# Stages 1 and 3 of a DFT in blocks of three instead of two, in a kernel of spectral mixing and hash-routed experts

## The chip, the cores and the metric

One NeuronCore of a Trainium2 chip runs the whole program. The metric is device time in microseconds for one execution. TensorE (PE in the profile) multiplies matrices: the stationary operand is loaded by a weight load (PEld), the moving operand streams through in columns, and the result lands in PSUM. VectorE (DVE), ScalarE (ACT) and GpSimd (POOL) do the other arithmetic. SyncE (SP), ACT and POOL issue DMAs; all DMAs run on the core's 16 DMA engines.

## The reference

```python
def _attn_ref(x, filt_r, filt_i):              # x: (8, 2496, 256) float32
    X = np.fft.rfft(x, axis=1)
    F = (filt_r + 1j * filt_i)[None, :, :]     # (1249, 256)
    return np.fft.irfft(X * F, n=x.shape[1], axis=1).astype(np.float32)

def _moe_ref(x, token_ids, w1, w2):            # x: (19968, 256), 8 experts, F = 1024
    expert_idx = token_ids * np.int64(2654435761) % np.int64(8)
    for e in range(8):
        mask = expert_idx == e
        out[mask] = np.maximum(x[mask] @ w1[e], 0.0) @ w2[e]
    return out
```

The first function's output, reshaped to 19968 tokens, is the second function's x. Everything is float32.

## The kernel before, in words

**The transform.** The length 2496 is split as 39 x 64 (N1 = 39, N2 = 64). The position in the sequence is s = 64 n1 + n2, and each batch goes through three stages (class `Batch`, lines 160 to 254).

- Stage 1 (lines 177 to 188) is a DFT of 39 points over n1, for each n2. Its input is real, so 20 frequencies with a real and an imaginary part (40 rows) come out. A matrix of 39 x 40 is small for an array of 128 x 128, so two blocks of n2 (n2 below 32 and from 32 on) are put on the diagonal of one stationary matrix `wf_t` of 78 x 80. A piece `u` (eight of them per batch) loads `x` for four values of n2 in each block (line 175, one DMA, 78 rows of 4 KB), does two products of 512 columns (line 185, two n2 times 256 channels each), copies them out of PSUM on ACT (line 187) and stores them to a DRAM buffer `d1` laid out as 40 x 64 x 256 (line 188).
- Stage 2 (lines 190 to 235) loads `d1` back with n2 on the rows (line 194), two DMAs per group of four frequencies, multiplies by a matrix that holds twiddles and the 64-point DFT (`pb`, line 202), by the filter (line 207, DVE), by the inverse matrix (`pc`, line 221), copies on ACT and stores to a second DRAM buffer `d2` of the same layout (line 228). There are 10 steps of forward and 10 of inverse work per batch.
- Stage 3 (lines 237 to 254) loads `d2` (line 239), does the inverse 39-point DFT with the 80 x 78 matrix `wi_t` (line 249), copies on DVE into a tile `o` (line 251) whose last 16 columns hold the token's number (an iota on POOL, line 245), and scatters one n2 at a time: 78 token rows per indirect DMA (line 257), four per piece and 32 per batch, to their places in the expert-sorted buffer `xs`. The index of each row stands in `sidx`.

A float32 product is two matmul instructions in the profile, each with its own weight load.

**Routing.** Early on, DVE and small matmuls count the tokens per expert, give each token a slot and write the slots to DRAM (line 403), from where they come back as `sidx` (line 404).

**Experts.** 163 tiles of 128 token rows follow. For tile i the kernel issues the load of tile i + 4's rows (line 519, SP), does the first layer (`up`, line 538), then conditional loads of the next weights (lines 283 and 285, SP), the transposes of tile i + 1 (line 527), then pieces of the transform that are due, then the second layer (`down`, line 550) and the scatter of the results (line 554, POOL).

**The order.** It is written by hand. Lists of (due time, piece) are sorted: `pre` (lines 491 to 496) runs before the first expert tile, and `main` (lines 498 to 504) is consumed tile by tile (lines 572 and 573), with due times in tiles. `part1` and `part3` (lines 462 and 479) spread the NU pieces of a stage evenly over a stretch of due times and issue each piece's load 1.9 steps ahead. Before the first expert tile run stage 1 of batches 0 to 2, stage 2 of batches 0 to 2 and stage 3 of batches 0 and 1; stage 1 of batch 3 and stage 3 of batch 2 come in the first six tiles, and the rest follows until tile 101. The expert tiles come in four groups that need the tokens of 2, 4, 6 and 8 batches. Buffers: three for `x`, two for `t1`, four for `t2`, three for `t4`, two for `o`, four PSUM tiles for all transform products. Each engine's and each queue's instructions run in the order in which they are written.

Of the kernel before, what the change touches and what calls it, by code (L numbers as in the profile page):

```python
# [19 lines left out]
P = 128  # L20
# [5 lines left out]

N1, N2 = 39, 64
NS, NQ = N1 // 2 + 1, 64
NR = 2 * N1
NK = 4 * NS  # L30
SG = 4
XG = 4
NU = N2 // 2 // XG
# [27 lines left out]
def dft_tables():  # L61
# [4 lines left out]
    wf = np.zeros((N1, 2, 2, NS, 2))  # L66
    wi = np.zeros((2, NS, 2, N1, 2))
# [27 lines left out]
def route_table():  # L95


    t = np.zeros((P, G + 2 + NQP), np.float32)
    p = np.arange(P)
    for g, b in enumerate(STAGES):  # L100
# [3 lines left out]
    t[:, G + 2:] = p[:, None] * NQP + np.arange(NQP)  # L104
    return t
# [3 lines left out]
def kernel(  # L109
# [42 lines left out]
    sidx = keep.tile([NR, B, N2 // 2], I32)  # L152
# [7 lines left out]
    class Batch:  # L160
# [8 lines left out]
        def rows(self, base, u):  # L169
            return bass.AP(tensor=base.tensor, offset=base.offset + (self.b * S + XG * u) * C,  # L170
                           ap=[[32 * C, NR], [C, XG], [1, C]])

        def load1(self, u):
            self.x[u] = xpool.tile([NR, XG, C], F32, name=f"x_{self.b}_{u}", tag="x")
            nc.sync.dma_start(out=self.x[u][:], in_=self.rows(x, u))

        def stage1(self, u):
            if self.d1 is None:
                self.d1 = dpool.tile([2 * NS, N2, C], F32, name=f"d1_{self.b}", tag="d1")
                self.d1_rows = self.d1.rearrange("a (h n) c -> (a h) n c", h=2)  # L180
            xt = self.x.pop(u)
            t1 = t1pool.tile([NK, XG, C], F32, name=f"t1_{self.b}_{u}", tag="t1")
            for i in range(XG // 2):
                ps = fps.tile([P, 2, C], F32, name=f"pa_{self.b}_{u}_{i}", tag="f")
                nc.tensor.matmul(out=ps[0:NK], lhsT=wf_t[:], rhs=xt[:, 2 * i:2 * i + 2, :],  # L185
                                 start=True, stop=True)
                nc.scalar.copy(out=t1[:, 2 * i:2 * i + 2, :], in_=ps[0:NK])  # L187
# [22 lines left out]
        def back(self, u):  # L210
            if self.d2 is None:
                self.d2 = dpool.tile([2 * NS, N2, C], F32, name=f"d2_{self.b}", tag="d2")
                self.d2_rows = self.d2.rearrange("a (h n) c -> (a h) n c", h=2)
# [23 lines left out]
        def load4(self, u):  # L237
            self.t4[u] = t4pool.tile([NK, XG, C], F32, name=f"t4_{self.b}_{u}", tag="t4")
            nc.sync.dma_start(out=self.t4[u][:], in_=self.d2_rows[:, XG * u:XG * u + XG, :])

        def stage3(self, u):

            t4 = self.t4.pop(u)
# [3 lines left out]
            for i in range(XG // 2):  # L247
                ps = fps.tile([P, 2, C], F32, name=f"pd_{self.b}_{u}_{i}", tag="f")
                nc.tensor.matmul(out=ps[0:NR], lhsT=wi_t[:], rhs=t4[:, 2 * i:2 * i + 2, :],  # L249
                                 start=True, stop=True)  # L250
                nc.vector.tensor_copy(out=o[:, 2 * i:2 * i + 2, 0:C], in_=ps[0:NR])  # L251
# [44 lines left out]
    rt = rpool.tile([P, G + 2 + NQP], F32)  # L296
    nc.scalar.dma_start(out=rt[:], in_=r_dram.ap())
    nc.scalar.dma_start(out=d_t[:], in_=d_dram.ap())
# [29 lines left out]
    def count():  # L328
# [26 lines left out]
        rv.update(mask=mask, run=run, ends=ends, ps=ps)  # L355

    def route():
# [36 lines left out]
        for g in range(1, G):  # L394
# [4 lines left out]
        slot = rpool.tile([P, NJ], F32)  # L399
        nc.vector.tensor_reduce(slot[:], acc[:].rearrange("p e j -> p j e"), axis=AX.X, op=OP.add)  # L400
        slot_i = rpool.tile([P, NJ], I32)
        nc.vector.tensor_copy(slot_i[:], slot[:])
        nc.gpsimd.dma_start(out=slot_dram[:].rearrange("(p j) -> p j", p=P), in_=slot_i[:])
        nc.gpsimd.dma_start(out=sidx[:], in_=slot_dram[:].rearrange("(b p n) -> p b n", b=B, p=NR))
# [13 lines left out]
                                       rt[:, G + 2:], op0=OP.mult, op1=OP.add)  # L418
        some = rpool.tile([P, NQP], F32)
        for e in range(E):  # L420
            nc.vector.tensor_scalar(some[:], rt[:, G + 2:], prior[:, e:e + 1], held[:, e:e + 1],
# [183 lines left out]
```

## Time and profile before

| what | value |
|---|---|
| median of 3 runs | 1742.96 us (1742.59 to 1743.45) |
| profiled execution | 1736.04 us |
| its span, first to last instruction | 1734.3 us |
| mean granted TensorE clock | 0.981 |
| DMA traffic | 260.72 MB, mean 150 GB/s |

The profile is one execution. Busy time is the union of an engine's instructions; a matmul's end is modelled, so its separate duration overlaps its neighbour's, and the distance between starts or the chain of waits is the better measure of what one costs. The chain is followed back from the last instruction, at each step to what released it. Stretches are counted from the first instruction.

### The profile page before, as it was taken

The numbers are of one execution on the slowest core, as the hardware profiler recorded it, in microseconds if no ns is written. First come the engines' busy times: TensorE is split into PE (matmuls) and PEld (weight loads), VectorE is DVE, ScalarE is ACT, GpSimd is POOL, SyncE is SP. The second block draws the span as 40 slices with busy tenths as digits, with TensorE's granted clock in tenths as the row PEclk, the third lists the DMA queues.
The fourth block names the chain that finished last, engine by engine and source line by source line (L and its number), as shares of the span: only waits on it lengthen the run. The fifth ranks groups of instructions, "written<-read, shape, count | busy, mean of one in ns | idle before, by whom it ended". The sixth has DMA issues, their size and how long they took to land.

```text
span 1734.3 us, 27336 instructions
## 1 busy us (share of the span) xinstructions
PE 1658.3 (96%) x9630; PEld 1390.2 (80%) x9630; DVE 462.6 (27%) x848; ACT 223.0 (13%) x373; POOL 428.3 (25%) x509
## 2 busy tenths in 40 slices
PE   5889869899999999999999999999999999999998
PEld 1455537588778888888888988888899999999997
DVE  8133412222332222222232232222222222222221
ACT  1322011121111111111110100000000000000000
POOL 1116434200233023321232222333321111111111
PEclk9999969899999999999999999999999999999999
DMA  9889755655766585375463554443516222222220
GB/s 249 230 204 318 202 145 170 168 158 157 218 199 174 160 239 183 93 210 131 118 189 103 176 179 131 130 129 119 163 43 232 87 87 86 86 84 85 84 82 11
DMA packets 158098, 260.72 MB, mean 150 GB/s; under 512 B 18271, under 2 KB 120192, under 8 KB 157643
## 3 DMA queue, kind: packets, MB, share of 16 engines
q1 hardware_dynamic: 108459, 166.93, 33.8%
q0 software_dynamic: 21168, 48.63, 8.7%
q10 hardware_dynamic: 28336, 43.43, 8.7%
q8 instruction: 77, 1.26, 0.3%
q14 instruction: 58, 0.48, 0.1%
HBM read 433.78 MB, written 86.09 MB: 300 GB/s over the span
## 4 chain that ended last, share of the span: by engine, by line
PE 64%; issue 24%; DMA 7%; POOL 4%; DVE 0%; POOLq 0%; SPq 0%; ACT 0%; ACTq 0%; DVEq 0%
PE ups L538 20%; PE dps L550 20%; PE pc L221 7%; PE pa L185 6%; PE pd L249 6%; PE pb L202 4%; POOL out_dram L554 4%; DMA x<-in_x_dram 2%; PE xps L527 1%; DMA w<-in_moe_w_dram 1%; DMA xs<-o,sidx 1%; DMA t<-d 1%; POOL xs L257 1%; DMA d<-g 1%; DVE o L251 0%
## 5 line engine op out<-in xcount | busy, mean ns | idle before, releaser
L538 PEld LDWEIGHTS ups<-xt,w 128*128 128x128 f32 x5216 | 610.5, 193 | 9.3 <-DVE xt L529 0.9
L538 PE MATMUL ups<-xt,w 128*128 128x128 f32 x5216 | 611.2, 276 | 0.5 <-DVE xt L529 0.5
L550 PE MATMUL dps<-w,ht 128*128 128x256 f32 x2608 | 591.8, 380 | 0.0
L550 PEld LDWEIGHTS dps<-w,ht 128*128 128x128 f32 x2608 | 490.5, 191 | 86.0 <-issue 24.5
L554 POOL DMA_INDIRECT out_dram<-osb,xg x163 | 159.9, 981 | 856.9 <-DVE osb L553 836.7
L257 POOL DMA_INDIRECT xs<-o,sidx x256 | 241.0, 942 | 399.9 <-issue 260.7
L544 DVE TENSOR_SCALAR ht<-ups 128x512 f32<-128x512 f32 x163 | 112.7, 691 | 525.7 <-PE ups L538 525.7
L542 ACT ACTIVATE ht<-ups 128x512 f32<-128x512 f32 x163 | 97.3, 597 | 1031.0 <-PE ups L538 1001.3
L553 DVE COPY osb<-dps 128x256 f32<-128x256 f32 x163 | 69.2, 424 | 507.7 <-PE dps L550 503.2
L185 PE MATMUL pa<-x,wf_t 78*80 78x512 f32 x256 | 144.8, 697 | 26.1 <-DMA x<-in_x_dram 26.0
L221 PE MATMUL pc<-p,e_t 128*128 128x256 f32 x640 | 154.6, 385 | 0.8 <-DVE p L207 0.8
L221 PEld LDWEIGHTS pc<-p,e_t 128*128 128x128 f32 x640 | 123.9, 194 | 21.7 <-DVE p L207 2.2
L207 DVE TENSOR_TENSOR p<-pb,filt 128x512 f32<-128x512 f32 x160 | 102.9, 685 | 113.5 <-PE pb L202 113.3
L249 PE MATMUL pd<-t,wi_t 80*78 80x512 f32 x256 | 125.8, 614 | 7.4 <-DMA t<-d 5.2
L185 PEld LDWEIGHTS pa<-x,wf_t 78*80 78x80 f32 x256 | 41.9, 171 | 91.9 <-issue 75.3
L251 DVE COPY o<-pd 78x512 f32<-78x512 f32 x128 | 87.2, 686 | 96.5 <-issue 41.4
L202 PE MATMUL pb<-t,d_t 128*128 128x256 f32 x320 | 89.0, 404 | 21.0 <-DMA t<-d 19.8
L202 PEld LDWEIGHTS pb<-t,d_t 128*128 128x128 f32 x320 | 61.8, 202 | 54.6 <-issue 39.3
L187 ACT COPY t<-pa 80x512 f32<-80x512 f32 x128 | 73.1, 581 | 183.7 <-PE pa L185 157.2
L249 PEld LDWEIGHTS pd<-t,wi_t 80*78 80x78 f32 x256 | 37.6, 153 | 57.7 <-issue 49.5
L224 ACT COPY g<-pc 128x512 f32<-128x512 f32 x80 | 46.8, 585 | 280.8 <-PE pc L221 255.3
L527 PE MATMUL xps<-ident,xg 128*128 128x128 f32 x326 | 62.5, 274 | 9.7 <-DMA xg<-xs 9.7
(80 smaller groups left out, 183.5 us busy)
## 6 DMA issues: line engine op xcount, KB each, us to landing
w<-in_moe_w_dram SPq DMA_DIRECT2D x326, 1024.0 KB
xg<-xs SPq DMA_DIRECT2D x163, 136.0 KB
d<-t ACTq DMA_DIRECT2D x64, 320.0 KB
t<-d SPq DMA_DIRECT2D x80, 256.0 KB
d<-g ACTq DMA_DIRECT2D x80, 256.0 KB
t<-d SPq DMA_DIRECT2D x64, 320.0 KB
x<-in_x_dram SPq DMA_DIRECT2D x64, 312.0 KB
xs<-o,sidx POOLq DMA_INDIRECT x256, 3.0
```

The lines of the kernel that those rows point to most:

```text
L185: nc.tensor.matmul(out=ps[0:NK], lhsT=wf_t[:], rhs=xt[:, 2 * i:2 * i + 2, :], start=True, stop=True)
L202: nc.tensor.matmul(out=ps[:, i, :], lhsT=d_t[:, s, :], rhs=self.t2[s // SG][:, s % SG, :], start=True, stop=True)
L207: nc.vector.tensor_tensor(out=pt[:], in0=ps[:], in1=f_t[k][:, 2 * u:2 * u + 2, :], op=OP.mult)
L221: nc.tensor.matmul(out=ps[:, i, :], lhsT=e_t[:, k, 2 * u + i, :], rhs=pr[k][:, i, :], start=(k == 0), stop=(k == 1))
L249: nc.tensor.matmul(out=ps[0:NR], lhsT=wi_t[:], rhs=t4[:, 2 * i:2 * i + 2, :], start=True, stop=True)
L251: nc.vector.tensor_copy(out=o[:, 2 * i:2 * i + 2, 0:C], in_=ps[0:NR])
L257: st = nc.gpsimd.indirect_dma_start(out=xs[:], out_offset=bass.IndirectOffsetOnAxis(ap=index, axis=0), in_=rows, in_offset=None, bounds_ch ...
L538: nc.tensor.matmul(out=ps[:, k, :], lhsT=w1[:, dp, fp * P:(fp + 1) * P], rhs=xt[i][:, dp, :], start=(dp == 0), stop=(dp == DP - 1))
L542: nc.scalar.activation(out=dst, in_=ps[:], func=AF.Relu)
L544: nc.vector.tensor_scalar_max(dst, ps[:], 0.0)
L550: nc.tensor.matmul(out=ps[:], lhsT=ht[:, fp, :], rhs=w2[:, fp, :], start=(fp == 0), stop=(fp == FP - 1))
L554: st = nc.gpsimd.indirect_dma_start(out=out[:], out_offset=bass.IndirectOffsetOnAxis(ap=xg[i][:, C:C + 1].bitcast(I32), axis=0), in_=o[:], ...
```

## The change

Stages 1 and 3 work on three values of n2 at once instead of two: the diagonal has three blocks and the matrices are 117 x 120 and 120 x 117. The blocks are now neighbouring values, n2 = 3 j + h with h = 0, 1, 2 and j = 0 to 20; n2 = 63 is left over and is done alone, with the first block of the same matrix (39 x 40). A piece takes four values of j, so there are six pieces per batch: five of four j, and one of one j and the single n2, which does two products of 256 columns. `x` is loaded by one DMA per block (three per piece, 39 rows each), and by a fourth in the last piece. The DRAM buffers `d1` and `d2` have n2 first (64 x 40 x 256). So stage 2 loads and stores 64 rows of 4 KB, and stages 1 and 3 store and load 120 rows of up to four runs of 1 KB. Token numbers come from a table (`tokno`) by a tensor_scalar on POOL in place of the iota. `sidx` is twice as wide and is filled by three DMAs. Each scatter holds 117 rows (21 per batch) or 39 (one per batch). Stage 2's arithmetic, the due times of the lists and the expert part stay.

```diff
-NR = 2 * N1
-NK = 4 * NS
+H, HN = 3, 21
+NR = H * N1
+NK = 2 * H * NS
 SG = 4
 XG = 4
-NU = N2 // 2 // XG
+NU = (HN + XG) // XG
...
-    for h in range(2):
-        wf[:, h, :, :, h] = w
-        wi[:, :, h, :, h] = v.transpose(0, 2, 1) / S
+    for h in range(H):
+        wf[h, :, h] = w
+        wi[h, :, :, h] = v.transpose(0, 2, 1) / S
...
-    sidx = keep.tile([NR, B, N2 // 2], I32)
+    sidx = keep.tile([NR, B, N2], I32)
+    tokno = keep.tile([NR, HN + 1], F32)
...
         def load1(self, u):
-            self.x[u] = xpool.tile([NR, XG, C], F32, name=f"x_{self.b}_{u}", tag="x")
-            nc.sync.dma_start(out=self.x[u][:], in_=self.rows(x, u))
+            xt = self.x[u] = xpool.tile([NR, XG, C], F32, name=f"x_{self.b}_{u}", tag="x")
+            off, n = x.offset + self.b * S * C, min(XG, HN - XG * u)
+            for h in range(H):
+                nc.sync.dma_start(out=xt[N1 * h:N1 * h + N1, 0:n, :],
+                                  in_=bass.AP(tensor=x.tensor, offset=off + (H * XG * u + h) * C,
+                                              ap=[[N2 * C, N1], [H * C, n], [1, C]]))
+            if n < XG:
+                nc.sync.dma_start(out=xt[0:N1, n, :],
+                                  in_=bass.AP(tensor=x.tensor, offset=off + (N2 - 1) * C, ap=[[N2 * C, N1], [1, C]]))
+
+        def products(self, w, rows, cols, src, dst, copy, u, name):
+            last = XG * u + XG > HN
+            for i in range(1 if last else XG // 2):
+                ps = fps.tile([P, 2, C], F32, name=f"{name}_{self.b}_{u}_{i}", tag="f")
+                if last:
+                    for k, f in enumerate((H, 1)):
+                        nc.tensor.matmul(out=ps[0:cols * f, k, :], lhsT=w[0:rows * f, 0:cols * f],
+                                         rhs=src[0:rows * f, k, :], start=True, stop=True)
+                        copy(out=dst[0:cols * f, k, 0:C], in_=ps[0:cols * f, k, :])
+                else:
+                    nc.tensor.matmul(out=ps[0:cols * H], lhsT=w[:], rhs=src[:, 2 * i:2 * i + 2, :],
+                                     start=True, stop=True)
+                    copy(out=dst[:, 2 * i:2 * i + 2, 0:C], in_=ps[0:cols * H])
+
+        def pieces(self, d, t, u):
+            n = min(XG, HN - XG * u)
+            main = d[0:H * HN].rearrange("(j h) a c -> (h a) j c", h=H)
+            parts = [(main[:, XG * u:XG * u + n, :], t[:, 0:n, :])]
+            if n < XG:
+                parts.append((d[N2 - 1], t[0:2 * NS, n, :]))
+            return parts
...
         def stage1(self, u):
-                self.d1 = dpool.tile([2 * NS, N2, C], F32, name=f"d1_{self.b}", tag="d1")
+                self.d1 = dpool.tile([N2, 2 * NS, C], F32, name=f"d1_{self.b}", tag="d1")
...
-            nc.scalar.dma_start(out=self.d1_rows[:, XG * u:XG * u + XG, :], in_=t1[:])
+            self.products(wf_t, N1, 2 * NS, self.x.pop(u), t1, nc.scalar.copy, u, "pa")
+            for dram, chip in self.pieces(self.d1, t1, u):
+                nc.scalar.dma_start(out=dram, in_=chip)
...
                 nc.sync.dma_start(out=t2[64 * p:64 * p + 64, :, :],
-                                  in_=self.d1[a0:a0 + SG, :, :].rearrange("s n c -> n s c"))
+                                  in_=self.d1[:, a0:a0 + SG, :])
...
-                    nc.scalar.dma_start(out=self.d2[a0:a0 + SG, :, :].rearrange("s n c -> n s c"),
+                    nc.scalar.dma_start(out=self.d2[:, a0:a0 + SG, :],
                                         in_=self.g[64 * p:64 * p + 64, :, :])
...
         def load4(self, u):
-            nc.sync.dma_start(out=self.t4[u][:], in_=self.d2_rows[:, XG * u:XG * u + XG, :])
+            for dram, chip in self.pieces(self.d2, self.t4[u], u):
+                nc.sync.dma_start(out=chip, in_=dram)
 
         def stage3(self, u):
-            nc.gpsimd.iota(o[:, :, C:].bitcast(I32), pattern=[[1, XG], [0, W - C]],
-                           base=self.b * S + XG * u, channel_multiplier=N2 // 2)
...
-            for i in range(XG):
+            nc.gpsimd.tensor_scalar(o[:, 0:n, C:].bitcast(I32),
+                                    tokno[:, XG * u:XG * u + n].unsqueeze(2).to_broadcast([NR, n, W - C]),
+                                    float(self.b * S), None, op0=OP.add)
+            self.products(wi_t, 2 * NS, N1, self.t4.pop(u), o, nc.vector.tensor_copy, u, "pd")
+            for i in range(n):
                 j = XG * u + i
-                scatter(o[:, i, :], sidx[:, self.b, j:j + 1], f"xs_{self.b}")
+                r, k = (NR, H * j) if j < HN else (N1, N2 - 1)
+                scatter(o[0:r, i, :], sidx[0:r, self.b, k:k + 1], f"xs_{self.b}")
...
-        nc.gpsimd.dma_start(out=sidx[:], in_=slot_dram[:].rearrange("(b p n) -> p b n", b=B, p=NR))
+        for h in range(H):
+            n = N2 if h == 0 else H * (HN - 1) + 1
+            slots = slot_dram[:]
+            nc.gpsimd.dma_start(out=sidx[N1 * h:N1 * h + N1, :, 0:n],
+                                in_=bass.AP(tensor=slots.tensor, offset=slots.offset + h,
+                                            ap=[[N2, N1], [S, B], [1, n]]))
```

## Rows read from the trace of the kernel before

**Rows 1.** The page, part 1: busy time, share of the span, instructions.
```profile
PE 1658.3 (96%) x9630; PEld 1390.2 (80%) x9630; DVE 462.6 (27%) x848; ACT 223.0 (13%) x373; POOL 428.3 (25%) x509
```

**Rows 2.** Busy time by stretch: us, engines (instructions), TensorE clock, DMA share, GB/s.
```profile
0.00:55.00 55.00, 33.59 (x40) 8.98 (x40) 35.98 (x66) 13.03 (x18) 13.95 (x27) 1.00 0.91 250
55.00:105.00 50.00, 45.18 (x151) 29.96 (x152) 13.92 (x25) 15.98 (x26) 0.00 (x0) 1.00 0.79 203
105.00:184.00 79.00, 64.06 (x203) 38.00 (x203) 26.14 (x40) 16.22 (x28) 31.66 (x40) 0.91 0.94 271
184.00:235.00 51.00, 38.12 (x138) 24.18 (x138) 20.74 (x33) 5.27 (x9) 31.73 (x40) 0.92 0.71 187
235.00:335.00 100.00, 86.69 (x399) 60.43 (x400) 20.84 (x37) 13.47 (x23) 37.54 (x45) 0.84 0.60 170
335.00:1260.00 925.00, 925.00 (x5495) 789.97 (x5496) 252.31 (x456) 120.79 (x206) 246.90 (x289) 1.00 0.55 159
1260.00:1734.00 474.00, 465.70 (x3209) 438.67 (x3207) 92.67 (x192) 38.21 (x64) 66.51 (x69) 0.99 0.27 89
```

**Rows 3.** TensorE's waits: us in total, times, longest.
```profile
PE pa L185 <- DMA x<-in_x_dram: 26.0, 8, 5.9
PE pb L202 <- DMA t<-d: 19.8, 3, 8.3
PE xps L527 <- DMA xg<-xs: 9.7, 1, 9.7
...
PE pd L249 <- DVE o L251: 1.6, 1, 1.6
PE pb L202 <- DVE o L251: 1.2, 1, 1.2
```

**Rows 4.** Chain of waits, 120 to 262 us: start, us, what.
```profile
122.69 1.72 PE pa L185 x4
124.41 0.86 PE pb L202 x4
...
153.75 21.41 DMA w<-in_moe_w_dram
...
183.96 1.91 PE pd L249 x4
...
229.09 2.44 DMA xs<-o,sidx
...
231.74 2.15 DMA xg<-xs
...
241.71 4.71 DMA x<-in_x_dram
246.55 3.67 PE pa L185 x4
```

**Rows 5.** Same columns as rows 2, instructions of line 185, then of 249.
```profile
335.00:1260.00 925.00, 61.96 (x128) 19.04 (x128) 1.00 0.55 159
...
335.00:1260.00 925.00, 75.28 (x160) 22.45 (x160) 1.00 0.55 159
```

**Rows 6.** Issues on SP by line: shortest, median, longest ns; first, last start.
```profile
L175 SPq DMA_DIRECT2D x<-in_x_dram x64: 307/370/1250, 1.3 to 835.1; - x64
...
L194 SPq DMA_DIRECT2D t<-d x80: 573/610/1685, 54.8 to 999.3; - x80
```

**Rows 7.** Timeline of POOL, 180 to 250 us: start, us, instruction.
```profile
186.61 0.95 POOL L257 DMA_INDIRECT xs<-o,sidx  x1 [13.65 <-DVE o L251]
...
230.04 0.21 POOL L245 IOTA o<- 78x64 int32 x1
```

**Rows 8.** The page, part 5: busy us, mean ns, idle before.
```profile
L554 POOL DMA_INDIRECT out_dram<-osb,xg x163 | 159.9, 981 | 856.9 <-DVE osb L553 836.7
```

**Rows 9.** Chain of waits, 0 to 56 us.
```profile
9.60 18.94 DMA x<-in_x_dram
```

**Rows 10.** The page, part 3: packets, MB, share of 16 engines.
```profile
q10 hardware_dynamic: 28336, 43.43, 8.7%
```

More of the change, by code (lines that the diff above doesn't have):

```diff
@@ L95, in route_table @@
 def route_table():
-    t = np.zeros((P, G + 2 + NQP), np.float32)
+    t = np.zeros((P, G + 2 + NQP + HN + 1), np.float32)
     p = np.arange(P)
+    n1, j = np.arange(NR) % N1, np.arange(HN)
+    t[:NR, G + 2 + NQP:-1] = (N2 * n1 + np.arange(NR) // N1)[:, None] + H * j
+    t[:N1, -1] = N2 * np.arange(N1) + N2 - 1
     for g, b in enumerate(STAGES):
@@ L103, in route_table @@
     t[:, G:G + 2] = np.array(order).reshape(2, P).T
-    t[:, G + 2:] = p[:, None] * NQP + np.arange(NQP)
+    t[:, G + 2:G + 2 + NQP] = p[:, None] * NQP + np.arange(NQP)
     return t
@@ L181, in stage1 @@
-            xt = self.x.pop(u)
+                self.d1 = dpool.tile([N2, 2 * NS, C], F32, name=f"d1_{self.b}", tag="d1")
             t1 = t1pool.tile([NK, XG, C], F32, name=f"t1_{self.b}_{u}", tag="t1")
[L183 to L187, printed above, removed]
@@ L211, in back @@
             if self.d2 is None:
-                self.d2 = dpool.tile([2 * NS, N2, C], F32, name=f"d2_{self.b}", tag="d2")
-                self.d2_rows = self.d2.rearrange("a (h n) c -> (a h) n c", h=2)
+                self.d2 = dpool.tile([N2, 2 * NS, C], F32, name=f"d2_{self.b}", tag="d2")
             pr = self.p.pop(u)
@@ L238, in load4 @@
             self.t4[u] = t4pool.tile([NK, XG, C], F32, name=f"t4_{self.b}_{u}", tag="t4")
-            nc.sync.dma_start(out=self.t4[u][:], in_=self.d2_rows[:, XG * u:XG * u + XG, :])
+            for dram, chip in self.pieces(self.d2, self.t4[u], u):
+                nc.sync.dma_start(out=chip, in_=dram)
         def stage3(self, u):
-            t4 = self.t4.pop(u)
+            n = min(XG, HN + 1 - XG * u)
             o = opool.tile([NR, XG, W], F32, name=f"o_{self.b}_{u}", tag="o")
-            nc.gpsimd.iota(o[:, :, C:].bitcast(I32), pattern=[[1, XG], [0, W - C]],
-                           base=self.b * S + XG * u, channel_multiplier=N2 // 2)
[L247 to L251, printed above, removed]
-            for i in range(XG):
+            nc.gpsimd.tensor_scalar(o[:, 0:n, C:].bitcast(I32),
[3 more added lines that the diff above has]
+            for i in range(n):
                 j = XG * u + i
-                scatter(o[:, i, :], sidx[:, self.b, j:j + 1], f"xs_{self.b}")
+                r, k = (NR, H * j) if j < HN else (N1, N2 - 1)
+                scatter(o[0:r, i, :], sidx[0:r, self.b, k:k + 1], f"xs_{self.b}")
     def scatter(rows, index, group):
@@ L295 @@
     nc.scalar.dma_start(tok[:], tok_h.bitcast(I32).rearrange("(p j two) -> p j two", p=P, two=2))
-    rt = rpool.tile([P, G + 2 + NQP], F32)
+    rt = rpool.tile([P, G + 2 + NQP + HN + 1], F32)
     nc.scalar.dma_start(out=rt[:], in_=r_dram.ap())
+    nc.vector.tensor_copy(tokno[:], rt[0:NR, G + 2 + NQP:])
     nc.scalar.dma_start(out=d_t[:], in_=d_dram.ap())
@@ L353, in count @@
         nc.tensor.matmul(out=ps[:, 1, 0:E], lhsT=before[:], rhs=cnt[:], start=True, stop=True)
-        rv.update(mask=mask, run=run, ends=ends, ps=ps)
+        rv.update(eid=eid, eid_i=eid_i, mask=mask, run=run, ends=ends, ps=ps)
     def route():
@@ L417, in route @@
         nc.vector.scalar_tensor_tensor(at[:], first[:, G - 1, 0:1].to_broadcast([P, NQP]), float(TB),
-                                       rt[:, G + 2:], op0=OP.mult, op1=OP.add)
+                                       rt[:, G + 2:G + 2 + NQP], op0=OP.mult, op1=OP.add)
         some = rpool.tile([P, NQP], F32)
         for e in range(E):
-            nc.vector.tensor_scalar(some[:], rt[:, G + 2:], prior[:, e:e + 1], held[:, e:e + 1],
+            nc.vector.tensor_scalar(some[:], rt[:, G + 2:G + 2 + NQP], prior[:, e:e + 1], held[:, e:e + 1],
                                     op0=OP.is_ge, op1=OP.mult)
```

11 lines of the change are left out of this document (3 added, 8 removed).

## The prediction

> **What bounds the kernel now.** First the busy shares of the page: the reader is to see TensorE at 96% and no other engine above 27% [rows 1]. A share of the whole span hides stages, so next the busy times by stretch [rows 2]. From 335 us to 1260 TensorE is busy in all of its 925.00 us, at the full granted clock, with the DMA engines at 0.55. The last 474 us hold only expert tiles. Before 335 it is another kernel: 33.59 of 55 us, 45.18 of 50, 64.06 of 79, 38.12 of 51, 86.69 of 100, with the DMA share at 0.91, 0.79, 0.94, 0.71 and 0.60. Third, TensorE's own waits [rows 3]: eight for loads of x, three for the loads of stage 2, one for the first expert tile's rows. So columns taken off TensorE after 335 us come off the end, and before 335 they are worth what the loads allow. I sum five stretches of the front and one of the rest.
>
> **The price of a column.** One product is two matmul instructions of 512 columns. In the chain four of them (two products) of `pa` (78 by 80) take 1.72 us, and four of `pb` (128 by 128, 256 columns) 0.86 [rows 4]: 0.43 and 0.215 us each. Time follows the columns and not how much of the array is filled, so 117 by 120 should cost 0.43 too. At the lower clock (1.2 of 2.4 GHz) the same four take 3.67 [rows 4].
>
> **Stages 1 and 3 on TensorE.** Before, a batch and stage has 16 products, 32 x 0.43 = 13.76 us. After, five groups of two products and one last group of two 256-column products: 20 x 0.43 + 4 x 0.215 = 9.46 us. Saved: 4.30 us per batch and stage. After 335 us lie 128 instructions of stage 1 (four batches) and 160 of stage 3 (five) [rows 5]: 9 x 4.30 = **-38.7 us**, with no wait in that stretch to give it back to. Bounds: -43 if the separate busy rows (61.96/128 = 0.484) were the price, -30 if a shorter step lays some waits open.
>
> **235 to 335.** Here lie stage 1 of batch 3 and stage 3 of batch 2, by the order written in the kernel: -8.6. Against it: x comes as three transfers where one came. The x load after the first expert layer stands in the chain with 4.71 us [rows 4], and it is issued only when that layer lets SP go on. An issue of 78 runs takes 0.37 us and one of 256 runs 0.61 [rows 6]; 156 runs are 0.47 by interpolation (an estimate), so the third lands 1 us later: +0.9. The wait of up to 8.3 us for stage 2's load [rows 3] is a round trip store, load, product; fewer columns ahead of it don't shorten it. Sum **-7.7**, bounds -12 and -2.
>
> **184 to 235: GpSimd.** Here scatters set the pace. The first starts at 186.61 and the iota behind the last at 230.04 [rows 7]: 32 scatters and 7 iotas of 0.21 in 43.4 us, so 1.31 us a scatter of which 0.95 are busy, and TensorE then waits 9.7 us for the rows [rows 3]. After: 21 scatters of 117 rows and one of 39. A 128-row scatter to the output takes 0.981 us [rows 8] against 0.95 for 78 rows, so 117 rows cost 0.02 more. The iota becomes a tensor_scalar, which no row shows on this engine: between 0.21 (the iota) and 0.95 (a scatter), taken at 0.3, for the same 64 elements a row. 22 x 1.33 + 6 x 0.3 = 31 us. TensorE had some 40 us, from its product at 183.96 to 9.7 us before the rows land at 233.9 [rows 3, 4]; less 4.3 and 2.8 of waits for buffers that scatters hold (1.6 and 1.2 [rows 3]) it needs 33 and becomes the pace. After its last stage 3 product come a copy, two scatters instead of four, 2.44 us to land and 2.15 for the tile's load [rows 4]: the first expert tile starts near 222 instead of 234. **-12**, bounds -4 (TensorE's share alone) and -16.
>
> **55 to 105.** TensorE is dense, DMA 0.79 [rows 2]: stage 1 of batch 1 gives **-4.3**, bounds -6 and 0.
>
> **105 to 184.** 8.6 us of TensorE work goes, but DMA stands at 0.94 and 271 GB/s [rows 2], and the chain ends in the 21.41 us of the first expert weights [rows 4]. The bytes stay; what changes is how they are cut. x, stage 1's stores and stage 3's loads go from runs of 4 KB to 1 KB; stage 2's loads and stores go from 1 KB to 4 KB. No row tells the two sizes apart; GB/s over the DMA share by stretch lies between 203/0.79 = 257 and 89/0.27 = 330 [rows 2]. Before 235 us 20.8 MB get smaller runs (x of three batches at 2.56, five buffers of 40 x 64 x 1 KB at 2.62) and 14.4 MB larger (5.5 buffers). From 330 down to 257 the first cost +18 us, from 257 up to 330 the second give -12. I take **+2** and keep both ends.
>
> **0 to 55.** One x load stands in the chain with 18.94 us [rows 9], beside tables on the other queues (6.5 MB of filters and the two stage 2 matrices, 26 us at the 250 GB/s of [rows 2]). At the lower clock [rows 4] stage 1 of one batch needs 8 x 3.67 us of TensorE before and 5.5 x 3.67 after, 9 less. If instead the small runs wait until the tables are through, work starts at 26 us and ends near 50 with the last piece's load, still inside this stretch. **-1**, bounds -9 and +5.
>
> **Who distributes the runs.** Queue 10 counts 28336 packets [rows 10]; the kernel's own runs on it are 64 x 80, 80 x 256 and 3 x 128, or 25984, and the other 2352 are 16 for each of its 147 transfers. The Trainium skill, "DMA: Bandwidth & Descriptors", "Why a DMA increments its semaphore by 16 and not by 1", has a transfer run on the largest number of engines up to 16 that divides the slowest dimension of both sides. The count agrees for 80 and 64 rows. By that rule 39 rows use 13 engines, as 78 do, and 120 rows use 15 instead of 16, which would stretch the 13.1 MB that the front moves so from 47 to 50 us of DMA time, +3 us where it is exposed; my +2 for 105 to 184 doesn't rest on it. It would be otherwise if the three blocks stayed a dimension of their own (rival 3).
>
> **Costed at nothing.** The copies of ACT and DVE shrink with the columns, off the path. SP's issues grow by some 4 us a batch (15 x 0.47 + 4 x 0.3 for x instead of 8 x 0.37; 10 x 0.3 instead of 10 x 0.61; 5 x 0.91 + 0.4 instead of 8 x 0.34, from [rows 6], estimates). What queues behind them are the loads of stages 2 and 3, weights and tile rows, issued more than a step of their stage ahead; a batch takes some 185 us after 335. The extra table columns, `tokno` and the two more `sidx` loads lie in the first 55 us on DVE and GpSimd, before the first product of stage 3, and DVE is busy in 35.98 of those 55 us [rows 2]; uncovered they would cost about 3 us.
>
> **Sum.** -1 - 4.3 + 2 - 12 - 7.7 - 38.7 = -61.7 us. The profiled execution took 1736.04 (span 1734.3), so 1674.3; the median of the runs is 6.92 above the profiled one: **1681 us**.
>
> **Rivals.** (1) The front keeps its length. For it: DMA shares of 0.91 and 0.94 and 8 waits for x. 0 to 184 then costs the +18 - 12 = +6 of the runs and gains nothing, instead of -3.3, the scatters' stretch gives 4.3, 235 to 335 gives 2: 38.7 - 6 + 4.3 + 2 = -39, **1704**. (2) The front is not held by DMA but by TensorE and GpSimd: -6, -6, -8.6, -16, -12 (the clock stays up more often) and -38.7, -87: **1656**. Against it: those shares. (3) Slower: the three blocks stay outermost in the transfers between the stages, so that each runs on three engines. Place: stage 1's stores and stage 3's loads in the front. Price: 250/0.91 and 271/0.94 GB/s [rows 2] are about 280 at full share, 17.5 an engine; 13.1 MB on three engines are 250 us, the other 41.7 MB (54.8 by [rows 2]) on 16 are 149, 399 in all where the front has 235: +164, less some 46: about **1860**. It decides from four engines down. Against it: block stride and row stride fit, h and a are one run of 120 rows. (4) The change doesn't shorten the main part: each of its four batches gets the wait that batch 3 has, 8.3 us, and half of the 16 us that a granted clock of 0.84 over the 100 us from 235 loses [rows 2], the other half being the x load's: 4 x 16.3 = 65 us back, **1746**. For it: the lead is counted in steps and the steps carry less work. Against it: 925.00 of 925.00 busy, and lead times of 1.9 steps on steps a third longer.
>
> **Chances.** The forecast 57% (own range 1666 to 1694), rival 1 20%, rival 2 13%, rival 3 5%, rival 4 5%. A measurement of this kernel tells 0.2%, 3.5 us, from no change. Faster: the forecast, rivals 1 and 2 and a fifth of rival 4, 0.91; the same: 0.03; slower: rival 3 and the worse end of rival 4, 0.06. The range runs from half of rival 2's to past the middle of rival 1's: 1660 to 1709.
>
> **What would show it.** In the profile after: four instructions of `pa` and `pd` still 1.72 us in the chain (if 117 by 120 is slower, the price of a column is wrong); 192 matmul instructions a stage where 256 stand now; no TensorE idle after stage 2 of batch 3; the first expert tile near 222 less what the front gained; scatters 176 at about 0.97; DMA share before 184 us no higher than now. The forecast is wrong if TensorE shows idle time in the main part, if packets on queues 1 and 10 take much longer per byte, or if the first expert tile starts after 234.

## The result, and the profile after

The changed kernel takes 1691.43 us, the median of 4 runs (1682.49 to 1693.85), where the kernel before took 1743.2 on the same chip (4 runs): a ratio of 0.9692, 95% interval 0.9654 to 0.9729, about 52 us. Forecast were 1681, range 1660 to 1709. The profiled execution took 1689.87 (span 1687.8), 1.56 below the median, where the forecast made for a profiled execution was 1674.3.

The page of the kernel after, parts 1, 3 and 5, answering to [rows 1, 10, 8]:

```profile
PE 1576.4 (93%) x9502; PEld 1373.6 (81%) x9502; DVE 437.3 (26%) x817; ACT 201.5 (12%) x341; POOL 373.9 (22%) x415
...
q10 hardware_dynamic: 28112, 43.44, 8.9%
...
L284 POOL DMA_INDIRECT xs<-o,sidx x176 | 177.7, 1009 | 312.6 <-issue 221.9
```

TensorE has 82 us less to do in a span that is 46.5 us shorter, so 35 us of it came back as idle time, 24 of them ahead of 311.5 us and 11 behind. The stretches tell where: busy time by stretch of the kernel after, cut at the same events as [rows 2] (columns as there: TensorE's products, its weight loads, VectorE, ScalarE, GpSimd, granted clock, DMA share, GB/s).

```profile
0.00:55.00 55.00, 18.90 (x32) 7.43 (x32) 30.20 (x51) 9.84 (x14) 5.92 (x18) 0.89 0.87 238
55.00:107.00 52.00, 41.23 (x147) 29.24 (x147) 20.05 (x42) 14.13 (x23) 11.63 (x11) 0.82 0.83 226
107.00:184.00 77.00, 53.37 (x185) 35.88 (x184) 23.23 (x36) 12.51 (x23) 24.47 (x28) 0.87 0.97 278
184.00:223.00 39.00, 32.54 (x130) 23.70 (x129) 17.70 (x28) 5.86 (x10) 24.33 (x28) 0.96 0.74 206
223.00:311.50 88.50, 73.92 (x384) 56.69 (x382) 17.89 (x33) 10.78 (x19) 29.97 (x33) 0.90 0.72 203
311.50:1214.00 902.50, 890.42 (x5421) 781.75 (x5422) 235.53 (x436) 110.14 (x190) 212.42 (x231) 1.00 0.56 163
1214.00:1690.00 476.00, 466.05 (x3211) 438.96 (x3209) 92.74 (x192) 38.23 (x64) 65.16 (x67) 0.99 0.27 88
```

The sixth row is the one to see. In [rows 2] TensorE was busy in all 925.00 us of it; now 12 of 902.50 are idle. TensorE's waits name what is new there, first over the whole span (us in total, times, longest), against [rows 3]:

```profile
PE pa L198 <- DMA x<-in_x_dram: 43.4, 5, 24.8
PE pb L231 <- DMA t<-d: 24.9, 3, 13.9
PE pa L194 <- ACT t L196: 10.2, 8, 4.7
PE pd L198 <- DMA t<-d: 8.7, 1, 8.7
PE pd L194 <- DVE o L196: 6.4, 8, 1.3
PE xps L559 <- DMA xg<-xs: 5.2, 1, 5.2
```

and from 311.5 to 1214 us alone:

```profile
PE pb L231 <- DMA t<-d: 7.4, 1, 7.4
PE pd L194 <- DVE o L196: 4.0, 5, 0.9
PE pa L194 <- ACT t L196: 3.8, 4, 1.8
PE dps L582 <- DMA w<-in_moe_w_dram: 2.8, 2, 1.8
PE ups L570 <- DMA w<-in_moe_w_dram: 1.5, 1, 1.5
```

The 7.4 us of the first row end at 311.5, so they lie ahead of this stretch; the other four rows are its 12 idle us. Line 194 is the last group of stages 1 and 3: 7.8 us of waits for a copy. The chain of one such group (start, us, what) shows why:

```profile
291.45 0.71 PE pa L194 x2
292.15 0.02 issue
292.18 0.38 ACT t L196
292.56 0.04 issue
292.60 0.57 PE pa L194 x2
```

The group's second product, into the other half of the same PSUM tile, starts only after the copy of the first; the code puts that copy between the two.

The same events in each kernel give the stretches' lengths. The changed kernel was profiled three times on three chips (the second and third as neighbours of the experiments), and one execution's front is not another's, so all three stand here, in us less than before. A plus is a stretch that grew. The limits are, in order, with their times before: the start of stage 2 of batch 0 (59.8), its end (105.4), the start of stage 2 of batch 2 (176.9), the first expert tile (234.0) and the start of stage 2 of batch 3 (334.8).

| stretch | forecast | after | second | third |
|---|---|---|---|---|
| to stage 2 of batch 0 | -1 | -0.5 | +2.5 | -0.4 |
| 55 to 105 | -4.3 | +1.7 | -2.7 | -3.2 |
| 105 to 184 | +2 | -0.2 | -3.2 | -0.8 |
| 184 to 235 | -12 | -12.3 | -11.2 | -11.8 |
| 235 to 335 | -7.7 | -12.0 | -15.0 | -14.4 |
| from stage 2 of batch 3 on | -38.7 | -23.2 | -23.6 | -20.9 |
| span | -61.7 | -46.5 | -53.2 | -51.5 |

The kernel before was profiled on the first chip alone, so the second and third columns compare across chips; by the medians on one chip the change is worth 51.8, 45.3 and 61.0 us on the three. But two rows miss in the same way in all three: the fifth gains more, the sixth less. The sixth is the one to explain.

### The profile page after: what moved, and what is told of

It is laid out like the page before. It is cut to its first block, busy times and chain, and to the rows that moved or that the text cites. A ratio compares the mean times of both kernels' runs of the same rounds, so it can differ in the third digit from the quotient of the medians.

```text
span 1687.8 us, 26817 instructions
## 1 busy us (share of the span) xinstructions
PE 1576.4 (93%) x9502; PEld 1373.6 (81%) x9502; DVE 437.3 (26%) x817; ACT 201.5 (12%) x341; POOL 373.9 (22%) x415
## 3 DMA queue, kind: packets, MB, share of 16 engines
q10 hardware_dynamic: 28112, 43.44, 8.9%
## 4 chain that ended last, share of the span: by engine, by line
PE 60%; issue 26%; DMA 8%; POOL 4%; SPq 1%; DVE 0%; ACT 0%; POOLq 0%; ACTq 0%; DVEq 0%
PE ups L570 20%; PE dps L582 20%; PE pc L249 7%; PE pd L198 4%; POOL out_dram L586 4%; PE pb L231 4%; PE pa L198 4%; DMA x<-in_x_dram 2%; DMA t<-d 2%; DMA d<-t 1%; DMA w<-in_moe_w_dram 1%; PE xps L559 1%; PE pa L194 0%; SPq L223 0%; POOL xs L284 0%
## 5 line engine op out<-in xcount | busy, mean ns | idle before, releaser
L570 PEld LDWEIGHTS ups<-xt,w 128*128 128x128 f32 x5216 | 609.4, 192 | 11.1 <-DVE osb L585 1.8
L284 POOL DMA_INDIRECT xs<-o,sidx x176 | 177.7, 1009 | 312.6 <-issue 221.9
L198 PE MATMUL pa<-x,wf_t 117*120 117x512 f32 x160 | 87.3, 675 | 43.4 <-DMA x<-in_x_dram 43.4
L231 PE MATMUL pb<-t,d_t 128*128 128x256 f32 x320 | 87.4, 398 | 24.9 <-DMA t<-d 24.9
L198 PEld LDWEIGHTS pa<-x,wf_t 117*120 117x120 f32 x160 | 31.7, 209 | 73.6 <-issue 59.3
L198 PE MATMUL pd<-t,wi_t 120*117 120x512 f32 x160 | 78.1, 611 | 8.7 <-DMA t<-d 8.7
L200 DVE COPY o<-pd 117x512 f32<-117x512 f32 x80 | 55.2, 692 | 56.4 <-issue 38.2
L561 DVE COPY xt<-xps 128x256 f32<-128x256 f32 x163 | 67.6, 415 | 8.0 <-PE xps L559 8.0
L559 PE MATMUL xps<-ident,xg 128*128 128x128 f32 x326 | 62.5, 274 | 5.2 <-DMA xg<-xs 5.2
L200 ACT COPY t<-pa 120x512 f32<-120x512 f32 x80 | 45.8, 587 | 135.2 <-PE pa L198 124.5
```

Source lines behind the costliest of these rows:

```text
L198: nc.tensor.matmul(out=ps[0:cols * H], lhsT=w[:], rhs=src[:, 2 * i:2 * i + 2, :], start=True, stop=True)
L200: copy(out=dst[:, 2 * i:2 * i + 2, 0:C], in_=ps[0:cols * H])
L231: nc.tensor.matmul(out=ps[:, i, :], lhsT=d_t[:, s, :], rhs=self.t2[s // SG][:, s % SG, :], start=True, stop=True)
L284: st = nc.gpsimd.indirect_dma_start(out=xs[:], out_offset=bass.IndirectOffsetOnAxis(ap=index, axis=0), in_=rows, in_offset=None, bounds_ch ...
L559: nc.tensor.transpose(out=ps[:, dp, :], in_=xg[i][:, dp * P:(dp + 1) * P], identity=ident[:])
L570: nc.tensor.matmul(out=ps[:, k, :], lhsT=w1[:, dp, fp * P:(fp + 1) * P], rhs=xt[i][:, dp, :], start=(dp == 0), stop=(dp == DP - 1))
```

## The experiments

The kernel before takes 1730 to 1750 us by chip (medians 1743.2, 1733.55, 1730.48, 1749.82, 1748.79), so kernels are compared on one chip: the first four experiments share one, the fifth to eighth another, the ninth and tenth a third, and the last pair a fourth.

**The last group's copies behind both products.**

```diff
                     for k, f in enumerate((H, 1)):
                         nc.tensor.matmul(out=ps[0:cols * f, k, :], lhsT=w[0:rows * f, 0:cols * f],
                                          rhs=src[0:rows * f, k, :], start=True, stop=True)
+                    for k, f in enumerate((H, 1)):
                         copy(out=dst[0:cols * f, k, 0:C], in_=ps[0:cols * f, k, :])
```

> The changed kernel with one edit: in the last group of stages 1 and 3 both 256-column products are issued before their two copies; before, the second product stood behind the copy of the first, in the same PSUM tile. Theory: that copy is what the second product waits for. In the changed kernel's profile nine such groups after 311 us took 18.2 us of TensorE from start to start where their columns are worth 7.7, so about 10 us come back there and up to 3 more in front: 10 to 13 us less than the changed kernel (profile 1689.9, so 1677 to 1680). Rival: the small products are slow by themselves (a new size of weights between two others): no change, 1690, and the group still takes 1.9 to 2.1 us.

Measured: 1677.93 us, ratio 0.9681 (0.9657 to 0.9705). TensorE's waits in the profile of this kernel from 306.1 us, its start of stage 2 of batch 3, to 1214:

```profile
PE pb L232 <- DMA t<-d: 8.3, 1, 8.3
PE dps L583 <- DMA w<-in_moe_w_dram: 2.1, 1, 2.1
PE ups L571 <- DMA w<-in_moe_w_dram: 1.4, 1, 1.4
PE dps L583 <- DVE o L201: 0.8, 1, 0.8
```

Both rows of the last group are gone, and a group takes 1.08 us, so the theory holds and the rival (1.9 to 2.1) falls. From start to start the nine last groups of the main part took 18.15 us in the changed kernel and take 9.71 here; the part from stage 2 of batch 3 on is 1368.4 us long, where the changed kernel's three profiles have 1376.3, 1375.9 and 1378.6. It is so in every profile: the five kernels here that have the copies behind both products take 1364.2 to 1369.3 us for that part, the seven of three blocks that have not take 1373.6 to 1378.6. The changed kernel itself did not run on this chip; two pairs below, each with a further edit in it, give the time against it.

**The count of tokens ahead of stage 1**, on the same chip.

```diff
-    pre = part1(0, -100, -81) + [(-99, count), ...
+    pre = part1(0, -100, -81) + [(-100.5, count), ...
```

> The changed kernel with one edit: the token count with its two small products goes ahead of the first group of stage 1 in the order. Theory: the count's products stood behind that group, which waits until 24.8 us for x, so the slots came at 52.8 us instead of 36 and their index loads and blank rows ran beside stage 2's first loads and the first store of batch 1 (10.7 us to land), which cost a wait of 6.6 us for x at 71. Then the slots' write starts near 36 us, that wait is under 2 us, and the first expert tile starts 3 to 6 us earlier. Rival: the 1 KB runs fill the DMA engines there anyway: slots early, wait unchanged, time within 2 us.

Measured: 1685.15 us (0.9729, 0.9708 to 0.975), 7.2 above the kernel with the copies moved beside it. The slots are written at 35.9 instead of 52.8, the wait for x falls from 6.6 to 3.4 us, the first expert tile comes at 220.7 against 222.7, and stage 2 of batch 0 starts 2.3 later. It lies between theory and rival. And it shows little: the other two profiles of the unaltered changed kernel have a wait of 2.6 us at that place, and by the table a shift of 2 us in the front is what executions differ by anyway.

**x in runs of 4 KB again**, each block of rows together, and stage 1's store in three transfers for it, on the same chip.

```diff
-  offset=off + (H * XG * u + h) * C, ap=[[N2 * C, N1], [H * C, n], [1, C]]
+  offset=off + (HN * h + XG * u) * C, ap=[[N2 * C, N1], [C, n], [1, C]]
...
-            for dram, chip in self.pieces(self.d1, t1, u):
-                nc.scalar.dma_start(out=dram, in_=chip)
+            for h in range(H):
+                nc.scalar.dma_start(out=self.d1[HN * h + XG * u:HN * h + XG * u + n].rearrange("j a c -> a j c"),
+                                    in_=t1[2 * NS * h:2 * NS * h + 2 * NS, 0:n, :])
```

> The changed kernel with stage 1 in other blocks of three (n2 = 21 h + j instead of 3 j + h): x is read in runs of 4 KB again, by as many transfers of the same bytes, and each store of stage 1 becomes three transfers of 40 rows; stage 3 is as in the changed kernel. Theory: in the first 25 us each DMA engine serves the queues one run at a time, so that a 1 KB run of x waits behind a 10 or 20 KB row as a 4 KB run did, and x came at a quarter of the rate: the first product starts at 6 to 11 us instead of 24.8 and stage 1 of batch 0 ends 3 to 8 us earlier. Rival: the queues share by bytes, and the first product was late because 468 KB are asked for instead of 312: first product not before 18 us. The whole time is left open within 8 us either way, for the stores now take three issues each on ten engines.

Measured: 1699.97 us (0.9799, 0.9772 to 0.9825), 14.8 above the kernel with the count moved, the nearest one on this chip. TensorE's waits:

```profile
PE pa L198 <- DMA x<-in_x_dram: 33.0, 5, 17.4
...
PE pa L194 <- DMA d<-t: 9.5, 1, 9.5
```

The first product starts at 17.4 us: neither theory nor rival. A new wait of 9.5 us for a store eats what that gave, and stage 2 of batch 0 starts at 67.5. So larger runs bring the first x earlier, by less than was expected, and the two more stores a group that come with them cost more than that.

**Filters and matrices behind batch 0's x**, the copies moved as above, on the same chip.

```diff
-        nc.gpsimd.dma_start(out=f_t[k][32 * q:32 * q + 32, :, :], ...
+        nc.sync.dma_start(out=f_t[k][32 * q:32 * q + 32, :, :], ...
...
+  (-90, tables)
```

> Both edits together: the products of the last group ahead of its copies, and the filters, the inverse matrices of stage 2 and stage 3's matrix loaded from SP behind the x loads of batch 0 instead of from GpSimd at the start. Theory (the front's first 60 us are x behind tables): the first product starts at 5 to 9 us, stage 1 of batch 0 ends near 30, and stage 2 starts when the filters have landed and been copied, at 42 to 50 us instead of 59; the first expert tile 8 to 15 us earlier than without the move. Rival: the bytes up to stage 2 are the limit, in whichever order they come: stage 2 starts at 57 to 60 and the gain is that of the first edit alone.

Measured: 1677.07 us (0.9674, 0.9661 to 0.9687), as without this edit. The first product starts at 11.7 and stage 1 of batch 0 is done at 32.5, and then TensorE waits for batch 1's x:

```profile
PE pa L199 <- DMA x<-in_x_dram: 41.3, 4, 22.8
```

Stage 2 starts at 62.5, later even than the rival's 57 to 60, and the time is the rival's. That the bytes are the limit fits this (14.4 MB moved in the first 62 us of the changed kernel, 14.9 here), but the edit doesn't show it alone: it also puts batch 1's x behind the tables in SyncE's queue, and the written order has batch 1's first piece ahead of stage 2. What is shown is that this order moves the wait, and not the end.

**The changed kernel again**, on another chip, beside the next three.

> The changed kernel once more, unaltered, on the chip of the runs beside it, so that they have their own base: 0.969 of the kernel before (0.965 to 0.973) if the ratio carries from chip to chip. If the spread of its first four runs (1682 to 1694) is its own, the runs here lie some 10 us apart as well.

Measured: 1685.19 us (0.974, 0.9726 to 0.9753). That is just above the 0.965 to 0.973 expected; the runs lie 4 us apart, not 10. It is the second profile of the table.

**Copies and count together**, beside it.

```diff
+                    for k, f in enumerate((H, 1)):
...
+    pre = part1(0, -100, -81) + [(-100.5, count), ...
```

> The changed kernel with the last group's products ahead of its copies and the token count ahead of stage 1's first group. Theory (two separate losses): the 8.4 us of the last groups and the 2 to 5 us of the late slots add up: 10 to 14 us less than the changed kernel beside it. Rival (the wait for x at 71 us comes and goes by itself, since it was also gone with the first edit alone): no better than the first edit alone, 8 to 11 us less.

Measured: 1678.29 us (0.9694, 0.9679 to 0.9709), 6.9 below the changed kernel, intervals apart: less than theory (10 to 14) and rival (8 to 11) had it. From stage 2 of batch 3 on it takes 1365.4 against 1375.9, -10.5 in these profiles; the front 304.2 against 305.2. So the rival is nearer: the gain lies where the copies are, and the count adds nothing that can be seen.

**A longer GpSimd stage**: the tensor_scalar of each group six times.

```diff
+            for _ in range(6):
+                nc.gpsimd.tensor_scalar(o[:, 0:n, C:].bitcast(I32), ...
```

> The changed kernel with the tensor_scalar that writes the token numbers done six times instead of once (the same values): 6 x 5 x 0.37 = 11 us more GpSimd time per batch, about what the change took away with ten scatters less. Theory (GpSimd's time set the pace between 184 and 235 us): the first expert tile starts 6 to 11 us later, at 229 to 234 in the profile, and the whole time grows by as much, for later batches hide it behind expert tiles. Rival (the loads of stages 2 and 3 set the pace there): the tile starts at 222 to 225 and the time is the same within 2 us.

Measured: 1698.56 us (0.9818, 0.9803 to 0.9833), 13.4 above the changed kernel beside it, and the first expert tile at 231.9 instead of 219.4. GpSimd's group in the page of this kernel:

```profile
L275 POOL TENSOR_SCALAR o<-tokno 117x64 int32<-117x64 f32 (+1 forms) x288 | 103.5, 359 | 23.6 <-DMA xs<-o,sidx 2.0
```

Five more of 0.36 us for the six groups of batch 1, whose stage 3 lies ahead of the first tile, are 10.8 us. Stage 2 of batch 2 starts 2.5 us later than in the changed kernel, and from there to the tile it is 55.9 us instead of 45.9. The theory holds: GpSimd paces that stretch after the change too, for nearly all that it got to do more shows in the length.

**x in twice the transfers**, same bytes and runs.

```diff
-                nc.sync.dma_start(out=xt[N1 * h:N1 * h + N1, 0:n, :], ...
+                for lo in range(0, n, 2):
+                    m = min(2, n - lo)
+                    nc.sync.dma_start(out=xt[N1 * h:N1 * h + N1, lo:lo + m, :], ...
```

> The changed kernel with each x load of two or more columns cut in two: 34 transfers of x per batch instead of 19, the same bytes and runs. Theory (the number of transfers is what costs: SP and ACT use eight DMA semaphores in turn, and an issue waits for the earlier transfer on its semaphore, so weights are issued late): the second expert layer after 311 us, which took 546.7 us from start to start against 542.2 before the change, grows by 3 us or more, and the whole time by 4 to 12. Rival (runs or bytes cost, not transfers): within 2 us of the changed kernel beside it.

Measured: 1699.45 us (0.9828, 0.9813 to 0.9843), 14.3 slower, and all of it ahead of stage 2 of batch 3, which starts at 319.2 instead of 305.2. TensorE's waits for expert weights from 343 to 1214 us hardly move, 4.4 against 4.2 us in the changed kernel beside it:

```profile
PE dps L584 <- DMA w<-in_moe_w_dram: 3.7, 3, 2.4
...
PE ups L572 <- DMA w<-in_moe_w_dram: 0.7, 1, 0.7
```

That part of the theory falls: it is not the number of x's transfers that makes the weights late. In the front they cost: the rival (within 2 us) falls too, and the 14.3 are more than the theory's 4 to 12.

**The new layout with the old blocks of two.**

```diff
-H, HN = 3, 21
+H, HN = 2, 32
...
-NU = (HN + XG) // XG
+NU = HN // XG
```

> The changed kernel with H = 2 and 32 values of j (n2 = 2 j + h): the buffers between the stages laid out by n2 first, 1 KB runs, x in a transfer per block and numbers from the table as in the changed kernel, but two blocks of 78 by 80, 16 products per batch and stage and 32 scatters. This is the layout without the third block. Theory (the gain is all from columns and scatters, the layout costs in front): 0 to 10 us slower than the kernel before, the first product at 12 to 20 us, the first expert tile at 234 to 244, and no waits for weights behind expert layers after 335, since tiles are as long as before. Rival (the layout's order of runs itself pays, in stage 2's 4 KB transfers): faster than before by 5 us or more. If the waits for weights of 1 to 2.5 us show here too, they come from the runs and not from shorter tiles.

Measured: 1746.23 us against 1749.82 before, ratio 0.9979 (0.996 to 0.9998). TensorE's waits from 343 to 1214 us:

```profile
PE pb L231 <- DMA t<-d: 8.7, 1, 8.7
PE dps L582 <- ACT ht L574: 1.4, 1, 1.4
```

The 3.6 us less are neither the theory (0 to 10 slower) nor the rival (5 or more faster). Runs of 1 KB where there were 4, and 4 where there was 1, are worth 0.4% at most by the interval, the other changes of layout included. No wait for weights shows either, so these come with the third block (shorter steps, larger transfers) and not with the runs alone.

**Weights behind the front's loads**, with copies and count as above, same chip.

```diff
-    pre += [(-30 + i, lambda i=i: (weights(i, 0), weights(i, 1))) ...
+    pre += [(-12 + i, lambda i=i: (weights(i, 0), weights(i, 1))) ...
```

> The changed kernel with the last group's products ahead of its copies, the count first, and the first two tiles' weights (4 MB) loaded behind stage 2's and stage 3's last loads of the front instead of ahead of them. Theory (in the stretch from 107 to 184 us the chain ends in those 4 MB, not in TensorE): stage 2 of batch 2 starts at 160 to 165 instead of 171.6 and the first expert tile 5 to 9 us earlier, 1669 to 1673 where the same kernel without the move took 1678 on another run of the chip. Rival (all DMA bytes of the front are the limit): the weights then delay stage 3's loads and the tile rows; first tile within 2 us of 218, time within 3 us.

Measured: 1671.19 us (0.9543, 0.952 to 0.9567). From its chain, 145 to 225 us, and from SyncE's timeline:

```profile
165.22 4.95 DMA t<-d
...
191.82 14.46 DMA t<-d
```

```profile
188.62 1.01 SPq L313 DMA_DIRECT2D w<-in_moe_w_dram  x1
191.82 6.33 SPq L269 DMA_DIRECT2D t<-d  x2
```

Stage 2 of batch 2 starts at 161.8 instead of 171.6, as the theory had it, but the first tile comes at 216.1, 2.3 earlier only, as the rival had it. The time is the theory's number, but the kernel without the move ran on another chip, so it says nothing. Nor is the rival shown. The edit doesn't do what it was to do: with due times of -12 and -11 the weights stand behind all loads of stage 2, but the load of stage 3's last group is due at -10.7. So this load is issued right behind the 4 MB, and it is the one that stands in the chain with 14.46 us. Weights behind that load too were not tried.

**The changed kernel, and all three edits beside it.**

> The changed kernel unaltered, as base for the run beside it: 0.969 to 0.974 of the kernel before, as on the two chips so far.

> The kernel of the run before last once more (last group's products ahead of its copies, count first, first weights behind the front's last loads), now on the same chip as the changed kernel. Theory: the edits are worth 8 us (last groups), 0 to 3 (count) and 2 (weights; the first expert tile came at 216.1 instead of 218.4): 10 to 14 us less than the changed kernel beside it. Rival: the front's DMA bytes make the last two worthless: 8 us or less.

Measured: 1687.83 (0.9652, 0.9625 to 0.9679) and 1673.71 (0.9573, 0.9548 to 0.9598), 14.1 us apart, intervals apart too. (The changed kernel's 0.9652 is below the 0.969 to 0.974 expected: on three chips its ratio differs by almost 1%.) The time is the theory's (10 to 14), the place is not. The profiled executions are 11.1 us apart: from stage 2 of batch 3 on it is 14.4 us less (1364.2 against 1378.6), where the copies are, and the front is longer, 307.4 against 304.2. So neither the count nor the move of the weights is shown to add anything.

## Why the prediction was right, and where its sum was off

**Direction and size.** The time fell for the reasons given: columns off TensorE, at the same price, and in one stretch scatters off GpSimd. In the chain of the kernel after, 120 to 345 us, against [rows 4]:

```profile
124.12 1.72 PE pa L198 x4
125.84 0.86 PE pb L231 x4
...
222.74 0.67 PE xps L559 x2
...
230.26 4.59 DMA x<-in_x_dram
```

Four instructions of 117 by 120 take 1.72 us as four of 78 by 80 did. The blocks-of-two kernel shows the other side: without the fuller array the layout gives next to nothing.

**"9 x 4.30 = -38.7 us", the term that was mis-sized.** It came out as -23.2, -23.6 and -20.9. Failed is the step "one last group of two 256-column products", priced at 4 x 0.215 = 0.86 us, 7.7 for nine, "with no wait in that stretch to give it back to". The nine took 18.15: 7.8 of waits for the copy between the two products, and 10.35 from start to start without them. With the copies behind, 9.71 remains, 0.27 an instruction instead of 0.215. That is 10.4 of the 15.5 us missing in the first profile. Another 4.3 us are the waits for expert weights, which [rows 3] has none of; their cause isn't settled. It is not the number of x's transfers and not the runs alone; shorter steps remain, and larger transfers (480 KB between the stages where there were 320), and neither was tried by itself. The result lies outside the forecast's own bound of -30, "if a shorter step lays some waits open", and idle time of TensorE in the main part was what the forecast itself named as showing it wrong. The copy was in the diff and could have been read there.

**Where luck helped.** In the first profile the rows ahead of stage 2 of batch 3 sum to -23.3 us, forecast -23.0. But some of them missed by 6.5 us in all one way and others by 6.8 the other way, so that the sum came out is luck; in the other two profiles, against a kernel before on another chip, it is -29.6 and -30.6.

**"235 to 335: -7.7".** It gave -12 to -15, the amount in rival 2. The clock is what the sum left out. Of this stretch TensorE was busy at the lower of its two levels (1.2 of 2.4 GHz) for 23.7 us before, and for 13.1, 8.6 and 6.8 us in the three profiles after; half of the difference is 5.3, 7.6 and 8.4 us given back. With them the sum is -13.0, -15.3 and -16.1, where -12.0, -15.0 and -14.4 came out. Why the clock rose earlier was not tested. The x load there was priced well: TensorE waited 5.43 us for it instead of 4.81, +0.6 where +0.9 was forecast.

**"184 to 235: -12"** held in all three (-12.3, -11.2, -11.8). The timeline of GpSimd, 184 to 224 us, first and last scatter and the tensor_scalar behind, answers to [rows 7]:

```profile
186.47 1.04 POOL L284 DMA_INDIRECT xs<-o,sidx  x1 [20.33 <-DVE o L200]
...
217.79 0.92 POOL L284 DMA_INDIRECT xs<-o,sidx  x1 [0.30 <-DMA xs<-o,sidx]
218.78 0.37 POOL L274 TENSOR_SCALAR o<-tokno 117x64 int32<-117x64 f32 x1
```

22 scatters in 32.3 us, where 31 were worked out, and the first tile at 222.7 where 222 was. One step of it was wrong: it made TensorE the pace there. The kernel with the longer tensor_scalar shows that GpSimd still is. The two estimates were near: a scatter takes 1.009 us (0.97 forecast), the tensor_scalar 0.374 (0.3).

**"55 to 105: -4.3".** +1.7 in the first profile, where x was late at 71 us; -2.7 and -3.2 in the other two. SyncE's timeline in the first one, 52 to 72 us, and ScalarE's store:

```profile
59.19 10.64 SPq L223 DMA_DIRECT2D t<-d  x2
69.93 1.50 SPq L179 DMA_DIRECT2D x<-in_x_dram  x3
```

```profile
58.44 0.34 ACTq L217 DMA_DIRECT2D d<-t  x1
```

Two issues of stage 2's load take 10.64 us, 9.7 of it between the two, and the loads of x queue behind them. In the trace's semaphore events the second one counts on the same semaphore as ScalarE's store of 58.44 us, which belongs to the next batch and lands at 69.19; the issue goes out at 69.38. TensorE's wait at this place is 6.6 us here, 2.6 in the other two profiles and 1.80 in the kernel with the copies moved. Why it comes and goes isn't settled; the forecast had no term for it.

**"0 to 55" and "105 to 184".** The first product started at 24.8 us, as the branch "if the small runs wait until the tables are through" had it (26), and stage 2 of batch 0 no later than before. The -1 came out within 4 us. Its reason, that the loads hold this stretch, is borne out as far as the kernel with the tables behind x goes; that it is their bytes alone is not shown. The forecast priced TensorE's work here at the lower clock, although [rows 2] has 1.00, and it was right to: the traces have no record of the clock ahead of 73 us before and 29 us after, and four instructions of `pa` take 3.69 us there before and 3.74 after. The stretch from 105 stayed within 2 to 5 us of the +2, nearer to a small gain; its DMA share went from 0.94 to 0.97, where the forecast wanted it no higher, and TensorE's waits for stage 2's loads in all from 19.8 to 24.9 us. Neither end of the price of small runs (+18, -12) showed: in the whole time of the blocks-of-two kernel they nearly cancel, and by stretch no run tells them apart.

**Who distributes the runs.** Queue 10 has 28112 packets. The kernel's own runs on it are again 25984, and the other 2128 are 48 x 15 + 8 x 10 + 83 x 16: 15 for each store of 120 rows, 10 for each of 40, 16 for the rest. The Trainium skill, "DMA: Bandwidth & Descriptors", "Why a DMA increments its semaphore by 16 and not by 1", gives the number of engines by the largest divisor up to 16 that the slowest dimensions of both sides share; the count agrees for 120 and 40 rows as it did for 80 and 64. Rival 3 needed three engines and falls.

**The other rivals.** Rival 1 (1704) wanted the front to keep its length: it became 23 to 31 us shorter. Rival 4 wanted a round trip's wait for each batch of the main part; there is one, batch 3's, with 7.4 us where it was 8.3. Rival 2 was right on 235 to 335 only.

## What to carry to other kernels

Price the remainder of a blocking by its order of instructions and not by its columns: here a short last group, two small products in one PSUM tile with the copy of the first between them, gave back a quarter of what had been counted on in the main part. When work leaves an engine that was busy in 100% of a stretch, look in that stretch for what becomes late next, and for what the clock gives back in the stretches that were not dense. When a piece is moved in a list of due times, see what is still due behind it. And take several profiles of a front that is limited by transfers before a term of a few us is called right or wrong: of one kernel, three profiles gave +1.7, -2.7 and -3.2.

## What was not expected of the hardware

The start of the first product depends on how x's first group is cut: 5.9 us with 78 runs of 4 KB (before), 17.4 with 117 of 4 KB, 20.5 with 312 of 1 KB (blocks of two), 24.8 with 468 of 1 KB. The time doesn't go by the bytes alone, which are 312 KB in the first and third, 468 in the others. With the tables' loads behind x, the same 468 runs were there at 11.7: it was beside those loads that they came late.

The time of an issue doesn't follow the number of its runs, though the forecast's interpolation took it so: the store of stage 1 with 480 runs has a median of 0.33 us on ScalarE, the load of stage 2 with 64 runs of 4 KB 0.552 on SyncE.

A 256-column product costs 0.264 to 0.276 us an instruction in the last groups, start to start, where four of `pb` in a row take 0.86.
